# Chunk-selected attention with a gated linear unit: the five-tap convolution on TensorE re-tiled to 64 x 32, and the selection mask applied in 64-row halves

## The chip, the cores and the metric

One core of a Trainium2 chip. The metric is the time of one execution on the device, in microseconds. Before the change it was 196.78 us in the median of three runs (196.16 to 199.24).

## What is computed

The first half is attention in which each query row may only look at six 32-row chunks of keys; the second half is a gated linear unit whose gate is a causal convolution over five rows. Cut to what matters (B, H, S, D = 4, 8, 768, 64; 24 chunks):

```python
ub = sum_d(max(q * k_min[chunk], q * k_max[chunk]))      # bound per query and chunk, causal chunks only
top_chunks = argsort(ub)[..., -6:]
mask = (chunk(j) in top_chunks) & (pos_i >= pos_j)
attn = softmax(where(mask, q @ k.T / 8, -1e9)) @ v
x = attn as [B, S, 512]                                  # the 8 heads side by side
gate = sigmoid(sum_k conv_w[k] * x shifted by k - 4)     # depthwise, five taps
out = (gate * (x @ w_val)) @ w_out
```

## The kernel before

**Pairs.** The 32 (batch, head) attention problems are done in 16 pairs: two heads share the 128 partitions, one in rows 0 to 63 and one in rows 64 to 127. Four pairs make one batch's 512 channels of `x`. For a pair p, in this order: `kn`, `qn`, `vn` are loaded (L517 to L526); K and Q are transposed on TensorE (L534) and copied to f16 as `Kh`, `Qh` by ScalarE (L540, L576); VectorE takes the chunks' minima and maxima (L546); GpSimd makes `KB` of them (L566 to L571); TensorE multiplies the bounds (`ub`, L652 or L667); VectorE finds the sixth largest (`top`) and writes 1 where a chunk is *not* selected into `NS` (`cmp`, L712 to L719); TensorE transposes `NS` (L726), and the copy of that is `MT` (L732, L734).

**Scores.** `score` (L738 to L761) computes K x Q for a pair into banks of PSUM, one bank for each head and each of six column ranges (`BANKS`, in 24 causal 128-blocks), with contraction over 64 rows (L748), and adds a penalty to the chunks that are not selected by a second matmul with the constant `E` (L757). `DUO` takes two ranges at a time; `cmp` writes `NS` twice, 32 columns apart, so that `MT` holds two copies of each head's rows, and four mask matmuls of 32 rows x 128 columns can run for two heads and two banks. ScalarE takes the exponential (L766), GpSimd zeroes the upper triangle of diagonal blocks (L774), TensorE multiplies by V (L797), VectorE normalises into `on` (L805, L806), and a transposing DMA (L827) or, for the last pair, TensorE (L822) makes `xT`, channels on partitions.

**Convolution.** Each pair's convolution is a set of matmuls whose weights are diagonal matrices. `CONV = "QQQQQQQQQQQSSSSQ"` gives each pair one of two ways.
- Q (`convq`, L876 to L885; 12 pairs): weights as f16 high part and low part (m), so 2 x 5 taps; tiles of 64 x 64. `XQ` is `xT` with its two 64-row halves exchanged by two DMAs (L849), so that four tiles work at once; 40 matmuls of 384 columns.
- S (`conv`, L856 to L865; pairs 11 to 14): `xT` is written to a DRAM scratch (L839) and read back four times (L845), which puts four copies of a channel, two of them shifted by three rows, on neighbouring partitions; tiles of 128 x 32, two halves of 12 matmuls.

ScalarE takes the tanh (L889). The weights are made once: `WQ` by ten GpSimd products of 512 elements (L476), `WD` by four of 384 (L445), after small VectorE steps (L416 to L437, L459 to L472). `wval` and `wout` are loaded by two DMAs from GpSimd (`wbig`, L408 to L412).

**Second half.** Once a batch's four `xT` are there: `val` = x @ w_val (L913), `gv` = (tanh + 1) * val (L921), `out` = gv @ w_out (L937), its copy (L944, L947) and the store (L952).

**Order.** Nothing is ordered by hand. `graph` lists the operations with a cost, what they read and write, and a key (`PERIOD` x pair + `OFF` + `DELTA`); `Graph.schedule` runs a list scheduler over TensorE, ScalarE, VectorE, GpSimd and SyncE with eight PSUM banks; the kernel is emitted in the resulting order, engine by engine. `fill` adds dummy matmuls (L1011) in gaps of TensorE planned before 26 us. All loads, exchanges, scratch transfers and stores are issued in one order from SyncE, which stops at the first that has to wait. Buffers per name are in `NBUF` (kn, qn, vn 5; XS, XQ 3; xT 8).

Of the kernel before, what the change touches and what calls it, by code (L numbers as in the profile page):

```python
# [33 lines left out]
XN = S + 6  # L34

# [15 lines left out]

DUO = ((0, 1), (2, 3), (4, 5))
SCORE = [0.68, 0.70, 0.54]
# [3 lines left out]
for _bi, _segs in enumerate(BANKS):  # L57
    for _col, _jt, _q0, _n in _segs:
        for _i in range(_n // 128):
# [5 lines left out]
PERIOD = 12.9223  # L65
OFF = dict(wdg=199.168, wbig=-116.538, cw=-683.48, load=-91.162, ktr=-51.291, qtr=99.521, kev=-172.346,
           qev=175.061, ksm=-204.505, spl=464.719, vc=678.633, ub=-186.285, top=322.7, selT=-163.727,
           sc=-181.883, ex=-292.07, av=82.464, nrm=333.712, tox=-546.25, xs=-141.243, conv=13.848,
           tanh=-338.872, val=266.063, gv=171.155, out=288.504, ev=-184.148)
# [11 lines left out]
CONV = "QQQQQQQQQQQSSSSQ"  # L81

DELTA = dict(
    wdg=(-1.243, -0.346, -5.29, 3.059, -8.51, 0.295, -11.031, 1.615, 2.466, -0.239, -5.796, 0, -2.239, 11.59,
        -0.038, 0),
    wbig=(0, 0.188, -10.953, -0.19, 0.733, -1.414, -3.353, 1.285, -5.523, -4.485, 38.175, 5.823, 4.557,
        -13.478, 0.421, 0),
    cw=(-18.314, -8.891, -8.843, -0.026, -0.2, 7.762, 12.344, 5.613, 0.06, -2.242, -4.873, -3.047, -3.366,
        0.828, -9.749, -0.011),
    load=(0.214, -1.353, 0.394, -9.477, -20.991, -15.326, -0.566, -8.721, 0.066, -10.887, 23.08, 13.879, 6.207,  # L90
        -4.098, -7.797, -2.716),
    ktr=(3.721, -2.57, -4.059, 0.646, -13.55, 0, 0.055, -1.62, -0.373, 0.436, -1.532, 6.05, 2.065, 1.379, 2.36,
        0.267),
    qtr=(-5.316, -3.862, 0.606, 2.517, 0.494, 0.207, -0.25, -17.411, 1.198, 7.239, -4.482, 0.617, -1.715,
        -0.705, 1.938, 2.43),
    kev=(0, -2.085, -0.198, 0.772, 0.854, 1.732, -0.381, -2.561, 0.048, 6.873, -0.748, -3.931, -1.54, -5.598,
        0, 0),
    qev=(-0.006, -7.153, 2.8, -8.078, -1.913, -4.426, -6.52, -0.93, -1.584, 0.557, 6.224, 0.433, 0, 0.167,
        0.325, 1.843),
    ksm=(-0.516, 1.719, 1.719, 0, -8.166, 5.024, -7.553, -5.823, 0, -13.821, -3.788, 0, 0, 0, 6.169, -3.771),  # L100
    spl=(0, 0, 0.913, -1.823, 3.174, 0.698, 2.737, 0, -0.344, -1.736, -3.55, 8.03, 12.699, 0.056, 12.489, 1.296),
    vc=(-5.408, 8.102, -1.641, -3.236, -11.492, -2.331, -9.437, 2.42, -16.561, 6.032, 0, -2.029, 9.507, 2.124,
        11.374, 1.314),
    ub=(0, 5.87, -1.717, -6.846, -10.954, -7.75, -4.319, 18.215, 2.367, -3.332, -1.487, -3.834, 2.838, -3.08,
        -3.376, 6.316),
    top=(0.011, -14.157, -0.748, -6.694, 0, 1.128, -0.085, 25.804, -19.326, 6.323, 7.216, 7.115, 6.031, 0,
        17.873, -1.714),
    selT=(0.159, 4.322, -11.032, -3.664, 2.206, 2.91, 4.105, -0.067, 0, 2.718, -8.959, -6.512, 0.16, 8.002,
        -0.12, -1.732),
    sc=(2.402, 2.062, 3.966, 0.001, -31.282, -1.168, -3.404, 9.113, -1.06, 0.639, 4.728, -3.231, -1.122,  # L110
        -0.658, -0.515, 0.885),
    ex=(-2.337, 0.461, 5.963, 6.189, 0.222, 2.13, 5.144, 9.503, 6.939, 0.624, 0.959, -13.542, -6.471, -4.563,
        6.731, -4.322),
    av=(0.086, -0.585, 2.526, 2.997, -2.315, -1.993, -1.22, 0, 3.593, 0, 0.163, -0.487, -7.862, -6.595, 1.978,
        -0.201),
    nrm=(-6.208, 0.692, -9.254, 2.271, -0.558, 4.28, 2.998, -3.761, 1.41, 1.599, -8.131, 15.962, -6.789,
        -7.511, -3.999, -3.399),
    tox=(-0.124, 4.074, 0.356, 0.146, 0, -8.203, -3.783, -8.724, -14.631, -6.792, 4.598, -8.206, -0.922,
        -1.434, -0.461, 1.278),
    xs=(-2.03, -2.537, 6.003, -3.321, -6.852, 156.074, 8.152, -17.228, -0.596, 0.102, -1.967, -1.865, -3.351,  # L120
        -1.967, -6.798, 4.494),
    conv=(-1.279, -0.745, -0.991, 1.197, -2.443, 4.986, 5.472, 4.646, -0.942, 1.84, 7.166, -0.096, 2.503,
        -1.052, 4.405, 6.594),
    tanh=(2.324, 0.747, -0.277, -2.803, 0, -3.819, -9.599, -8.531, -3.417, -0.893, -3.327, -0.726, -11.212,
        -0.762, 0.19, -5.493),
    val=(9.122, 0, -6.241, -3.696, 12.326, 2.893, 6.691, -2.508, -1.856, -2.108, -6.259, 37.115, 3.96, 9.385,
        10.567, 13.154),
    gv=(0.221, -7.002, -6.129, -3.775, -3.838, 1.864, 0, 7.518, 5.786, 5.443, -1.952, 0.455, 3.175, 0.33,
        -10.961, 5.879),
    out=(1.189, 1.43, -6.802, 3.456, 1.001, 0.92, -7.795, 60.654, -9.234, 0.84, 0.994, -0.377, 1.598, -2.455,  # L130
        -0.186, 1.785),
    ev=(-3.564, -1.25, -5.306, -0.157, 0, -6.542, 10.476, 4.737, 0.526, 6.5, 7.77, 0.056, 0, 0.402, 3.529,
        -0.709),
# [186 lines left out]
def graph(off, period, nbuf):  # L320
# [81 lines left out]

    if "S" in CONV:
        def w_cw():
            t.nc.sync.dma_start(out=t.cw, in_=t.conv_w.rearrange("k (c d) -> (k c) d", d=32))
        G.op("cw", "SP", 0.6, key("cw", 1), w_cw, w=[("cw",)], lat=3.0)

    def w_big():  # L408
        t.nc.gpsimd.dma_start(out=t.wval, in_=t.w_val.rearrange("(ct c) e -> c ct e", c=128))
        t.nc.gpsimd.dma_start(out=t.wout, in_=t.w_out.rearrange("(et e) o -> e et o", e=128))  # L410
    later = []
    later.append(G.op("wbig", "POOL", 2.4, key("wbig", 2), w_big, w=[("wbig",)], dma=6.4))  # L412

    if "S" in CONV:
        def w_rep():
            t.nc.vector.tensor_copy(out=t.cw4, in_=t.cw.unsqueeze(2).to_broadcast([80, 32, 4]))  # L416
        G.op("cwrep", "DVE", 0.6, 11.4, w_rep, r=[("cw",)], w=[("cw4",)])

        def w_tr():
            t.nc.tensor.transpose(out=bank("cwT")[:, 0:80], in_=t.cw4.rearrange("p d b -> p (d b)"),  # L420
                                  identity=t.ident[0:80, 0:80])
        G.op("cwT", "PE", 0.12, 11.4, w_tr, r=[("cw4",), ("ident",)], ps=["cwT"])

        def w_split():
            nc, b = t.nc, bank("cwT")
            v, c4 = nc.vector, t.ident.rearrange("p (c b) -> p c b", b=4)
            v.tensor_reduce(out=t.pm[:, 0:4], in_=t.ident.rearrange("p (c b) -> p b c", b=4), axis=AX.X, op=ALU.add)
            v.tensor_reduce(out=t.id4, in_=c4, axis=AX.X, op=ALU.add)
            v.tensor_tensor(out=t.pm[:, 4:6], in0=t.pm[:, 0:2], in1=t.pm[:, 2:4], op=ALU.add)
            v.tensor_tensor(out=t.pm[:, 6:7], in0=t.pm[:, 0:1], in1=t.pm[:, 1:2], op=ALU.add)  # L430
            v.tensor_tensor(out=t.pm[:, 7:8], in0=t.pm[:, 2:3], in1=t.pm[:, 3:4], op=ALU.add)
            v.tensor_copy(out=t.whi, in_=b[:, 0:80])
            v.tensor_tensor(out=t.wlo, in0=b[:, 0:80], in1=t.whi, op=ALU.subtract)
            v.tensor_scalar(out=t.wlo, in0=t.wlo, scalar1=t.pm[:, 5:6], scalar2=None, op0=ALU.mult)
            v.scalar_tensor_tensor(out=t.wlo, in0=t.whi, scalar=t.pm[:, 4:5], in1=t.wlo, op0=ALU.mult, op1=ALU.add)
            v.tensor_scalar(out=t.wsel, in0=t.wlo[:, 0:48], scalar1=t.pm[:, 6:7], scalar2=None, op0=ALU.mult)
            v.scalar_tensor_tensor(out=t.wsel[:, 0:32], in0=t.wlo[:, 48:80], scalar=t.pm[:, 7:8], in1=t.wsel[:, 0:32],  # L437
                                   op0=ALU.mult, op1=ALU.add)
        G.op("wsplit", "DVE", 2.7, 11.4, w_split, r=[("cwT",), ("ident",)], w=[("wsel",)], ps=["cwT"],
             after=[G.ops[-1]])  # L440

        def w_diag(j):
            def emit():
                sl = slice(12 * j, 12 * j + 12)
                t.nc.gpsimd.tensor_tensor(  # L445
                    out=t.WD[:, sl, :], in0=t.id4.unsqueeze(1).to_broadcast([128, 12, 32]),
                    in1=t.wsel[:, sl].unsqueeze(2).to_broadcast([128, 12, 32]), op=ALU.mult)
            return emit
        for j in range(4):
            G.op(f"wdiag{j}", "POOL", 0.8, 12.3 + 0.1 * j, w_diag(j), r=[("wsel",)], w=[("WD",)])  # L450

    if "Q" in CONV:
# [26 lines left out]
        for m in range(2):  # L479
            for k in range(KSZ):  # L480
                later.append(G.op(f"qdiag{m}{k}", "POOL", 1.0, key("wdg", 2, 0.5 * (m * KSZ + k)), q_diag(m, k), r=[("qw",)],
                                  w=[("WQ",)]))
# [659 lines left out]
```

## Time and profile before

| what | value |
|---|---|
| median of three runs | 196.78 us |
| profiled execution, its own time | 197.75 us |
| its span, first to last instruction | 196.0 us |
| ScalarE exponentials L766 | 192, 88.9 us busy |
| AV matmuls L797 | 672, 28.0 us busy |
| convolution Q matmuls L883 | 480, 21.8 us busy |
| convolution S matmuls L863 | 96, 4.7 us busy |
| K x Q matmuls L748 / mask matmuls L757 | 384, 28.8 us / 352, 17.6 us busy |
| GpSimd products for WQ / for WD | 10, 10.9 us / 4, 3.2 us busy |
| DMAs of kn, qn, vn | 32, 32 and 16, of 192, 192 and 384 KB |

A matmul's duration in the profile is counted until its last result is out, and matmuls overlap, so busy times of lines overlap too and cannot be added; the distance from one start to the next is what a matmul takes of TensorE. A row of tiles written "64*64 64x384" is a weight tile of 64 rows x 64 columns and a moving operand of 64 x 384.

### The profile page before, as it was taken

The numbers are of one execution on the slowest core, as the hardware profiler recorded it, in microseconds if no ns is written. First come the engines' busy times: TensorE is split into PE (matmuls) and PEld (weight loads), VectorE is DVE, ScalarE is ACT, GpSimd is POOL, SyncE is SP. The second block draws the span as 40 slices with busy tenths as digits, with TensorE's granted clock in tenths as the row PEclk, the third lists the DMA queues.
The fourth block names the chain that finished last, engine by engine and source line by source line (L and its number), as shares of the span: only waits on it lengthen the run. The fifth ranks groups of instructions, "written<-read, shape, count | busy, mean of one in ns | idle before, by whom it ended". The sixth has DMA issues, their size and how long they took to land.

```text
span 196.0 us, 7461 instructions
## 1 busy us (share of the span) xinstructions
PE 184.8 (94%) x2926; PEld 118.4 (60%) x2926; DVE 148.3 (76%) x476; ACT 146.7 (75%) x326; POOL 90.4 (46%) x189
## 2 busy tenths in 40 slices
PE   7989898979999999999999999999999997899992
PEld 3666666656757675686675677577656462555540
DVE  6897588979999988879998558998899614062451
ACT  4458999989778879895969897677988977633421
POOL 5589999888445344547262137414363212100000
PEclk9999999999999999999999999999999999999999
DMA  5999999989989998969796998230218839777225
GB/s 134 269 269 207 163 211 205 255 161 225 236 147 222 151 279 190 262 142 222 198 257 181 251 221 162 58 70 2 47 48 251 117 92 282 221 261 251 106 110 211
DMA packets 94917, 36.01 MB, mean 184 GB/s; under 512 B 88226, under 2 KB 91298, under 8 KB 94882
## 3 DMA queue, kind: packets, MB, share of 16 engines
q1 hardware_dynamic: 93826, 34.48, 74.5%
q0 software_dynamic: 1056, 1.05, 3.8%
q8 instruction: 23, 0.38, 0.8%
q14 instruction: 12, 0.10, 0.2%
HBM read 24.16 MB, written 7.08 MB: 159 GB/s over the span
## 4 chain that ended last, share of the span: by engine, by line
PE 74%; DVE 12%; DMA 5%; ACT 4%; SPq 2%; issue 2%; DVEq 0%
PE b L883 10%; PE b L913 10%; PE b L937 9%; PE b L797 9%; PE b L748 8%; PE b L534 8%; PE b L757 5%; PE b L652 5%; DMA xT<-on 3%; DVE km L546 3%; ACT P L766 2%; DMA XS<-scr 2%; PE b L726 2%; PE b L1011 2%; PE b L352 2%; DVE NS L716 2%
## 5 line engine op out<-in xcount | busy, mean ns | idle before, releaser
L766 ACT ACTIVATE P<-b 128x512 f16<-128x512 f32 (+1 forms) x192 | 88.9, 570 | 9.8 <-PE b L757 4.7
L774 POOL TENSOR_SCALAR_AFFINE_SELECT P<-P 128x512 f16<-128x512 f16 (+1 forms) x64 | 33.8, 550 | 60.5 <-ACT P L766 60.4
L546 DVE TENSOR_REDUCE km<-b 128x12 f32<-128x384 f32 x64 | 31.9, 548 | 6.7 <-PE b L534 2.8
L748 PE MATMUL b<-Qh,Kh 64*128 64x128 f16 (+3 forms) x384 | 28.8, 258 | 0.9 <-ACT P L766 0.4
L797 PE MATMUL b<-VA,P 128*128 128x65 f16 x672 | 28.0, 194 | 0.5 <-ACT P L766 0.4
L797 PEld LDWEIGHTS <-P 128*128 128x128 f16 x672 | 24.8, 98 | 4.1 <-issue 1.8
L921 DVE SCALAR_TENSOR_TENSOR gv<-g,b 128x384 f16<-128x384 f32 x32 | 17.5, 550 | 10.2 <-PE b L913 9.1
L913 PE MATMUL b<-xT,wval 128*128 128x384 f16 x128 | 23.8, 326 | 0.0
L937 PE MATMUL b<-wout,gv 128*128 128x512 f16 x96 | 23.5, 379 | 0.0
L947 ACT ACTIVATE osb<-b 128x512 f32<-128x512 f32 x21 | 12.8, 623 | 13.8 <-PE b L937 11.7
L889 ACT ACTIVATE g<-b 128x384 f32<-128x384 f32 x32 | 14.4, 495 | 10.2 <-PE b L883 7.6
L883 PE MATMUL b<-xT,WQ 64*64 64x384 f16 x240 | 21.8, 325 | 0.0
L883 PE MATMUL b<-XQ,WQ 64*64 64x384 f16 x240 | 21.8, 325 | 0.0
L540 ACT ACTIVATE Kh<-b 128x384 f16<-128x384 f32 x32 | 16.2, 520 | 7.0 <-PE b L534 5.2
L748 PEld LDWEIGHTS <-Kh 64*128 64x128 f16 x384 | 12.0, 94 | 12.8 <-issue 11.3
L806 DVE TENSOR_TENSOR on<-b,rcp 128x384 f16<-128x384 f32 x32 | 17.8, 557 | 1.1
L576 ACT ACTIVATE Qh<-b 128x384 f16<-128x384 f32 x32 | 15.7, 531 | 2.7 <-PE b L534 2.7
L757 PE MATMUL b<-MT,E 32*128 32x128 f16 (+4 forms) x352 | 17.6, 259 | 0.0
L883 PEld LDWEIGHTS <-WQ 64*64 64x64 f16 x480 | 12.8, 106 | 6.8 <-issue 2.0
L913 PEld LDWEIGHTS <-wval 128*128 128x128 f16 x128 | 11.5, 98 | 7.9 <-issue 1.3
L622 DVE SCALAR_TENSOR_TENSOR rl<-Qh,ql 128x640 f16<-128x640 f16 x16 | 15.9, 994 | 0.2
L534 PE MATMUL b<-ident,kn 128*128 128x128 f32 x96 | 15.1, 282 | 0.1
(102 smaller groups left out, 320.8 us busy)
## 6 DMA issues: line engine op xcount, KB each, us to landing
kn<-in_k_dram SPq DMA_DIRECT2D x32, 192.0 KB, 3.7
qn<-in_q_dram SPq DMA_DIRECT2D x32, 192.0 KB, 3.7
vn<-in_v_dram SPq DMA_DIRECT2D x16, 384.0 KB, 5.1
out_dram<-osb SPq DMA_DIRECT2D x24, 256.0 KB, 3.1
XS<-scr SPq DMA_DIRECT2D x16, 193.3 KB, 3.3
XQ<-xT SPq DMA_DIRECT2D x24, 96.8 KB, 2.5
scr<-xT SPq DMA_DIRECT2D x4, 193.5 KB
wval<-in_moe_w_val_dram POOLq DMA_DIRECT2D x1, 512.0 KB, 8.6
```

The costliest lines, as they stand in the source:

```text
L534: t.nc.tensor.matmul(out=b[:, j * 128:(j + 1) * 128], lhsT=vv(name, p)[:, 3 * w + j, :], rhs=t.ident, is_transpose=True, start=(j == 0), s ...
L546: t.nc.vector.tensor_reduce(out=vv("km", p)[:, i, w * 12:(w + 1) * 12], in_=bank(("kn", p, w))[:, 0:HB].rearrange("p (c t) -> p c t", t=CH ...
L748: t.nc.tensor.matmul(out=bank(("s", p, bi, hh))[:, col:col + n], lhsT=kh[HP[hh], jt * 128:(jt + 1) * 128], rhs=qh[HP[hh], q0:q0 + n], star ...
L757: t.nc.tensor.matmul(out=bank(("s", p, bi, hh))[:, col + m0 - q0:col + n], lhsT=t.E[rows, jt * 128:(jt + 1) * 128], rhs=mt[rows, m0 - 128: ...
L766: t.nc.scalar.activation(out=t.P[p % 2][hh][bi], in_=bank(("s", p, bi, hh))[:, 0:n], func=AF.Exp, scale=0.125 / QS)
L774: t.nc.gpsimd.affine_select(out=ap, in_=ap, pattern=[[0, n], [1, 128]], compare_op=ALU.is_ge, fill=0.0, base=0, channel_multiplier=-1)
L797: t.nc.tensor.matmul(out=b[:, qt, :], lhsT=t.P[p % 2][hh][bi][:, col:col + 128], rhs=vv("VA", p)[:, hh, jt, :], start=(jt == 0), stop=(jt ...
L806: t.nc.vector.tensor_tensor(out=vv("on", p)[:, :, hh * 64:(hh + 1) * 64], in0=b[:, :, 0:D], in1=rc.unsqueeze(2).to_broadcast([128, NT, D]) ...
L883: t.nc.tensor.matmul(out=bank(("cv", p, r))[HP[c], 0:HB], lhsT=t.WQ[HP[r], k // KSZ, k % KSZ, (p % 4) * 2 + c, :], rhs=x[HP[r], a:a + HB], ...
L913: t.nc.tensor.matmul(out=k[:, 0:HB], lhsT=t.wval[:, ct, et * 128:(et + 1) * 128], rhs=t.xT[:, (4 * b_ + ct) % 8, XL + w * HB:XL + (w + 1) ...
L921: t.nc.vector.scalar_tensor_tensor(out=vv("gv", 4 * b_ + et)[:, sl], in0=vv("g", 4 * b_ + et)[:, sl], scalar=1.0, in1=bank(("val", b_, et, ...
L937: t.nc.tensor.matmul(out=k, lhsT=vv("gv", 4 * b_ + et)[:, s * 128:(s + 1) * 128], rhs=t.wout[:, et, :], start=(et == 0), stop=(et == NCT - 1))
```

## The change

1. `CONV = "RRRRRRRRRRRRRRRQ"`: pairs 0 to 14 use a new way R. The DRAM scratch now holds 64 rows: 32 channel slots for each half of the 768 rows of `x`, so two writes; it is read back twice, into every second partition, so that each channel has two neighbouring rows (the weight's high part on one, its low part on the other). Five taps x four channel groups x two halves of the sequence make 40 matmuls of 384 columns in eight tiles of 64 x 32. `WD` is 80 blocks of 32 columns instead of 48; way S is gone. Pair 15 keeps Q, and `WQ` is made for that pair's two blocks alone.
2. The mask matmuls use the 64 rows of a head at once (tiles of 64 x 128, as K x Q), bank by bank, directly after their K x Q matmul; `DUO` is gone, and `cmp` writes `NS` once.
3. `wbig` is split into `wval` and `wout`, each with its own key, and not before `ksm3` and `ksm4`; `WQ`'s two products come after `ksm4`; the small weight steps have keys of their own.
4. `PERIOD`, `OFF`, `DELTA` and the planner's costs for the changed operations have other values, so that the order changes on every engine.

```diff
-CONV = "QQQQQQQQQQQSSSSQ"
+CONV = "RRRRRRRRRRRRRRRQ"
-DUO = ((0, 1), (2, 3), (4, 5))
...
-    later.append(G.op("wbig", "POOL", 2.4, key("wbig", 2), w_big, w=[("wbig",)], dma=6.4))
+        last.append(G.op(x, "POOL", 1.2, key("wbig", 2 + 2 * i), w_big, w=[(x,)], dma=3.0))
...
+        for j in range(KSZ):
+            later.append(G.op(f"wdiag{j}", "POOL", 1.0, key("wdg", 2, 0.5 * j), w_diag(j), r=[("wsel",)], w=[("WD",)]))
-                out=t.WQ[:, m, k], in0=t.id2.unsqueeze(1).to_broadcast([128, 8, 64]),
+                out=t.WQ[:, m], in0=t.id2.unsqueeze(1).unsqueeze(1).to_broadcast([128, KSZ, 2, 64]),
...
-            for r in range(2):
-                t.nc.vector.tensor_tensor(
-                    out=vv("NS", p).rearrange("p i (s c) -> p i s c", s=2)[:, :, :, CH * r:CH * r + NCH],
...
+            t.nc.vector.tensor_tensor(
+                out=vv("NS", p).rearrange("p i (s c) -> p i s c", s=2)[:, :, :, 0:NCH],
...
+        def score(bi, p=p):
...
+                for si, (col, jt, q0, n) in enumerate(segs):
...
+                    for hh in range(2):
+                        nc.tensor.matmul(out=bb[hh][:, col:col + n], lhsT=kh[HP[hh], jt * 128:(jt + 1) * 128],
...
+                    if masked:
                         for hh in range(2):
...
+                            nc.tensor.matmul(out=bb[hh][:, col + m0 - q0:col + n],
+                                             lhsT=t.E[HP[hh], jt * 128:(jt + 1) * 128],
+                                             rhs=mt[HP[hh], m0 - 128:q0 + n - 128], start=False, stop=last,
...
         def xw(p=p):
-            t.nc.sync.dma_start(out=t.scr[p % 4].rearrange("c (g n) -> g c n", g=4), in_=t.xT[:, p % 8, XL - 4:XL + S + 2])
+            for r in range(2):
+                t.nc.sync.dma_start(out=t.scr[p % 4][32 * r:32 * r + 32].rearrange("c (g n) -> g c n", g=4),
+                                    in_=t.xT[:, p % 8, XL - 4 + HB * r:XL + HB + HB * r])
         def xs(p=p):
-            for blk in range(4):
-                t.nc.sync.dma_start(out=vv("XS", p)[blk::4, 0:n - 3], in_=t.scr[p % 4][:, sh:sh + n - 3])
+            for blk in range(2):
+                t.nc.sync.dma_start(out=vv("XS", p)[blk::2, :], in_=t.scr[p % 4])
...
+        def conv(p=p):
+            x = vv("XS", p)
+            for k in range(KSZ):
+                for g in range(4):
+                    for r in range(2):
+                        t.nc.tensor.matmul(out=bank(("cv", p, r))[32 * g:32 * g + 32, 0:HB],
+                                           lhsT=t.WD[HP[r], k * 16 + (p % 4) * 4 + g, :],
+                                           rhs=x[HP[r], g * XH + k:g * XH + k + HB], start=(k == 0), stop=(k == KSZ - 1))
```

## The prediction

> **What bounds the kernel now.** I read the page first: shares of the engines and the slices.
>
> ```profile
> PE 184.8 (94%) x2926; PEld 118.4 (60%) x2926; DVE 148.3 (76%) x476; ACT 146.7 (75%) x326; POOL 90.4 (46%) x189
> ...
> PE   7989898979999999999999999999999997899992
> ...
> DMA  5999999989989998969796998230218839777225
> ```
>
> TensorE is nearly always busy, but busy includes the drain of each matmul, so I looked at stretches (columns: busy us of PE, PEld, DVE, ACT, POOL with instruction counts, clock, DMA share, GB/s).
>
> ```profile
> 20.00:50.00 30.00, 26.88 (x511) 18.65 (x511) 26.00 (x90) 28.59 (x68) 27.37 (x46) 1.00 1.04 202
> 50.00:75.00 25.00, 24.89 (x485) 17.70 (x484) 23.66 (x81) 19.48 (x45) 11.46 (x28) 1.00 0.99 206
> 100.00:125.00 25.00, 25.00 (x445) 16.17 (x443) 19.11 (x64) 19.57 (x45) 10.94 (x26) 1.00 0.81 192
> 125.00:150.00 25.00, 25.00 (x434) 16.37 (x433) 22.96 (x78) 21.42 (x49) 9.97 (x22) 1.00 0.31 73
> ```
>
> From 20 to 50 us ScalarE is full (28.59 of 30). From 50 to 150 TensorE is full to within 0.1 us of 100, about ten pairs at 10.0 us each. TensorE's waits agree: the longest, 2.0 us for `XS` from the scratch, comes at 167.5 us, and no other exceeds 1.3. So from 50 us to the end TensorE's own time counts. The timeline shows what a matmul takes of it, from start to start:
>
> ```profile
> 55.22 0.32 PE L883 MATMUL b<-xT,WQ 64*64 64x384 f16 x2
> ...
> 55.38 0.33 PE L883 MATMUL b<-xT,WQ 64*64 64x384 f16 x2
> ...
> 55.54 0.33 PE L883 MATMUL b<-xT,WQ 64*64 64x384 f16 x2
> ...
> 55.81 0.61 PE L748 MATMUL b<-Qh,Kh 64*128 64x512 f16 x4
> 56.34 0.39 PE L757 MATMUL b<-MT,E 32*128 32x512 f16 x4
> 56.67 0.45 PE L748 MATMUL b<-Qh,Kh 64*128 64x256 f16 x8
> 57.05 0.34 PE L757 MATMUL b<-MT,E 32*128 32x256 f16 x8
> ```
>
> A round of four 64 x 64 tiles takes 0.162 us (0.16 between the first rows), as long as 384 columns alone; so four tiles do run at once, 3 ns apart. But 55.54 to 55.81 is 0.26: about 0.095 more, and I find 0.09 to 0.10 at nearly every place where the tile shape changes (64 x 128 to 32 x 128: median 0.095 over 48). A way-S round (four tiles of 128 x 32) takes 0.166.
>
> Next the loads, from SyncE's timeline and TensorE's: pair 15's kn, qn, vn are issued here, and kn is first used at 140.82.
>
> ```profile
> 110.72 3.45 SPq L522 DMA_DIRECT2D kn<-in_k_dram  x2
> 115.46 1.27 SPq L522 DMA_DIRECT2D qn<-in_q_dram  x2
> 116.83 0.49 SPq L519 DMA_DIRECT2D vn<-in_v_dram  x1
> ```
>
> The second kn load lands by about 116, so the DMA side, full until 125 us, is 24 us ahead at the end, though only 3 to 7 us ahead (qn) at pairs 5 to 7.
>
> **What the skill says.** "TensorE: Matmul & The Clock Gate", Part 3, has tiles at different positions running concurrently, starts about 4 ns apart; sixteen 32 x 32 tiles gave 10.6 times. The trace agrees for four tiles (3 ns); no run here shows eight. "TensorEngine Tiling (Array Packing)", Tiling Modes, lists eight tiles of 64 x 32, and says that a change of mode, not of tile, drains the array: agreed, 0.095 us. "Trainium Kernel Development and Optimization", Key Constraints: DMAs from all queues share the same 16 engines. The trace agrees in that the share is 1.04 from 20 to 50 us, where `wval` and `wout` from GpSimd load beside SyncE's transfers.
>
> **The change, part by part,** on TensorE first.
>
> *Convolution.* Before: 12 Q pairs x 10 rounds x 0.162 = 19.4 us, 4 S pairs x 6 rounds x 0.166 = 4.0: 23.4. After: 15 R pairs x 5 rounds of eight tiles. No row shows one; bounds: 0.16 (384 columns, fully side by side; below that nothing) and 0.33 (only four at once, S's streams full). I take S's 0.165, since S already feeds four moving streams of 128 rows, as much data as eight of 64, and Q already loads as many weight columns per round (4 x 64 = 8 x 32). 75 x 0.165 = 12.4, plus pair 15's 1.6: 14.0. **-9.4 us.**
>
> *Masks.* Between 50 and 150 us the start-to-start times of L757 add up to 9.1 us for ten pairs; 30 of them end in a shape change (2.85), so 0.63 us a pair stream, four strips at once. After, two strips: the segments of the six banks sum to 320 + 448 + 512 + 512 + 384 + 256 = 2432 columns a head; 512 columns take 0.216 us in L937 (eight in 1.73 on the chain), so 1.03 us. +0.40 a pair, x16: **+6.4 us.** K x Q keeps its columns.
>
> *Shape changes.* Counted in the two built orders of TensorE: 160 before, 115 after (the 48 between K x Q and masks go; single score banks among other work add some). 45 x 0.095: **-4.3 us.**
>
> Sum on TensorE: -7.3 us. Before 50 us, where ScalarE is full, masks (+0.4 x 3.5 pairs) and shape changes nearly cancel and are covered by its waits there; everything of the convolution comes later. If TensorE's cover were gone before 50 us, that would cost 0.5.
>
> *VectorE.* `cmp` falls from 0.72 to about 0.36 us (two instructions to one): -5.8 over 16; the weight steps of 3 us before the first K reduction become about 2.3 later. Not on the path while TensorE is full, and it keeps VectorE's 23.66 of 25 us from becoming the bound: per pair 8.9 - 0.4 = 8.5 of 9.5 us, 89% as now.
>
> *GpSimd.* WQ and WD (10.9 + 3.2) become five products of 512 (1.11 each) and two of 640 (1.39 by size): 8.3; -5.8. Its 27.37 of 30 us before 50 loosens, as do ScalarE's waits for `KB` (2.9 us in all). I take 0; bounds -2.5 and 0. `wval` and `wout`, later, free DMA time (7.5 us) for the first loads and are needed only after 60 us.
>
> *DMA and SyncE.* Q costs 128 packets of 1548 B (0.10 us each over 16 engines: 0.8 us a pair). R writes 256 packets of 776 B and reads 128 of 3104 B: no row; by S's rates (1548 B at 15 GB/s, 6186 B at 21 per engine) 0.8 + 1.2 = 2.0 us; lower 1.5 (each at its undisturbed speed), upper 2.8 (all at the 13.4 GB/s of 256 B packets). I take 2.0. By the last qn load the new order on SyncE has sent 9.5 pairs' transfers, where 9 Q pairs' were sent before: 9.5 x 2.0 - 9 x 0.8 = 12 us later. Of the 24 us of lead, 12 and TensorE's 7 come off; 5 are left. So it is hidden, by that lead; at 2.8 us a pair it would be late by 2 to 3. SyncE issues 16 DMAs more (0.58 each, 9 us); it waits some 75 us now. Behind each scratch read, which waits for its write to land, loads and stores are queued; who waits is first `XS`, then pair 14's convolution: the new order puts about 16 us of matmuls between that pair's AV and its convolution, and transpose, write, read with their issues take 13 to 15 (before: 153.4 to 167.2 on the chain). I add 0.5 for such waits; bounds -2 (before's 2.0 vanishes) and +5.
>
> Sum against the profiled span: 196.0 - 7.3 + 0.5 = 189.2. The median of the runs lies 0.8 above the span (the profiled execution's own time 1.75), so 190.0 us.
>
> **Rivals.**
> 1. *Eight tiles run as four and four.* Nothing speaks against S's bandwidth, but no trace shows eight. Each round then takes 0.33, +12.4 us: 202.4, slower. It decides from a round of 0.256 (no change) and 0.31 (2% slower).
> 2. *The DMA side becomes the bound.* For: share 0.99 to 1.04 up to 75 us, leads of only 3 to 7 us there. Against: 24 us of lead at the end and `wval`, `wout` out of the first loads. With leads gone I price it at 5 us of waits: 195.
> 3. *VectorE or ScalarE keep the old pace.* For: VectorE 95% busy from 50 to 75. Against: -0.36 us a pair there. Half of TensorE's gain is lost: 193.5.
>
> **How the numbers follow.** Main course 0.57 (187 to 192.5 as its own range), rival 1 0.12, rival 2 0.17 (with a long tail), rival 3 0.14. About 2% (192.8, 200.7) is what a measurement of this kernel can tell from no change. Faster: 0.55 of the main course, a little of 2 and 3: 0.62. Slower: most of rival 1 and the tail of 2: 0.14. Same: 0.24. The range reaches from 185.5 (GpSimd's and the wait's lower bounds, -4) to 201: beyond lies most of rival 1.
>
> **What would show it.** Rounds of eight starts 0.16 to 0.17 us apart and 40 in 0.9; shape changes still 0.095; mask and K x Q of one bank with no gap; TensorE's start-to-start time full from 50 us with nearly no wait for `kn`, `qn` or `XS`. I am wrong if rounds take over 0.25, or if TensorE waits for loads after 60 us.

## The result

The kernel after takes 204.24 us in the median of four runs (203.45 to 205.55), the kernel before on the same chip 197.0: the ratio is 1.039, 95% interval [1.030, 1.048]. It is slower by 3.9%; 190.0 was predicted. The profiled execution took 204.88 us, with a span of 203.1.

Ratios here compare, for each kernel, the runs within about 1.5% of its fastest, so a ratio can lie below that of the two medians. Where I turn a difference of ratios into time, 1% is 1.97 us.

### The profile page after: what moved, and what is told of

Read it like the earlier page. It is cut to its first block, busy times and chain, and to the rows that moved or that the text cites. A ratio compares the mean times of both kernels' runs of the same rounds, so it can differ in the third digit from the quotient of the medians.

```text
span 203.1 us, 7574 instructions
## 1 busy us (share of the span) xinstructions
PE 180.6 (89%) x2981; PEld 120.9 (60%) x2981; DVE 142.1 (70%) x456; ACT 144.8 (71%) x326; POOL 86.1 (42%) x182
## 4 chain that ended last, share of the span: by engine, by line
PE 51%; DMA 19%; DVE 12%; ACT 10%; issue 3%; SPq 3%; ACTq 0%; DVEq 0%
DMA qn<-in_q_dram 12%; PE b L920 9%; PE b L896 8%; PE b L738 7%; PE b L525 7%; PE b L781 6%; ACT P L752 6%; PE b L743 5%; PE b L846 4%; DMA XS<-scr 4%; PE b L643 3%; DMA kn<-in_k_dram 2%; SPq L513 2%; ACT Qh L567 2%; DVE km L537 2%
## 5 line engine op out<-in xcount | busy, mean ns | idle before, releaser
L738 PE MATMUL b<-Qh,Kh 64*128 64x128 f16 (+3 forms) x384 | 39.4, 261 | 0.2
L743 PE MATMUL b<-MT,E 64*128 64x128 f16 (+4 forms) x352 | 37.3, 257 | 1.1 <-DVE MT L724 1.1
L781 PE MATMUL b<-VA,P 128*128 128x65 f16 x672 | 26.4, 193 | 0.0
L738 PEld LDWEIGHTS <-Kh 64*128 64x128 f16 x384 | 18.2, 95 | 12.4 <-issue 8.6
L896 PE MATMUL b<-xT,wval 128*128 128x384 f16 x128 | 25.3, 327 | 0.0
L930 ACT ACTIVATE osb<-b 128x512 f32<-128x512 f32 x21 | 12.8, 618 | 16.6 <-PE b L920 11.5
L630 POOL CAST VA<-vn 128x768 f16<-128x768 f32 x16 | 13.7, 866 | 21.7 <-DMA vn<-in_v_dram 12.2
L567 ACT ACTIVATE Qh<-b 128x384 f16<-128x384 f32 x32 | 15.5, 531 | 9.6 <-PE b L525 9.6
L743 PEld LDWEIGHTS <-E 64*128 64x128 f16 x352 | 17.7, 95 | 4.9 <-issue 2.1
L846 PE MATMUL b<-XS,WD 64*32 64x384 f16 x600 | 15.8, 341 | 4.2 <-DMA XS<-scr 4.2
L525 PE MATMUL b<-ident,qn 128*128 128x128 f32 x96 | 14.3, 280 | 5.5 <-DMA qn<-in_q_dram 4.7
L525 PEld LDWEIGHTS b<-ident,kn 128*128 128x128 f32 x96 | 11.3, 151 | 9.2 <-ACT P L752 5.7
```

The source lines that it names most:

```text
L525: t.nc.tensor.matmul(out=b[:, j * 128:(j + 1) * 128], lhsT=vv(name, p)[:, 3 * w + j, :], rhs=t.ident, is_transpose=True, start=(j == 0), s ...
L567: t.nc.scalar.activation(out=vv("Qh", p)[:, w * HB:(w + 1) * HB], in_=bank(("qn", p, w))[:, 0:HB], func=AF.Copy, scale=QS)
L738: nc.tensor.matmul(out=bb[hh][:, col:col + n], lhsT=kh[HP[hh], jt * 128:(jt + 1) * 128], rhs=qh[HP[hh], q0:q0 + n], start=(si == 0), stop= ...
L743: nc.tensor.matmul(out=bb[hh][:, col + m0 - q0:col + n], lhsT=t.E[HP[hh], jt * 128:(jt + 1) * 128], rhs=mt[HP[hh], m0 - 128:q0 + n - 128], ...
L781: t.nc.tensor.matmul(out=b[:, qt, :], lhsT=t.P[p % 2][hh][bi][:, col:col + 128], rhs=vv("VA", p)[:, hh, jt, :], start=(jt == 0), stop=(jt ...
L846: t.nc.tensor.matmul(out=bank(("cv", p, r))[32 * g:32 * g + 32, 0:HB], lhsT=t.WD[HP[r], k * 16 + (p % 4) * 4 + g, :], rhs=x[HP[r], g * XH ...
```

## The profile after

First the page of the kernel after: shares, slices of TensorE, of its clock and of the DMA engines.

```profile
PE 180.6 (89%) x2981; PEld 120.9 (60%) x2981; DVE 142.1 (70%) x456; ACT 144.8 (71%) x326; POOL 86.1 (42%) x182
...
PE   7899899997969589989699999979976999799992
...
PEclk9999999999999889999889999999997999999999
DMA  7999999999876799996999997988979862728055
```

TensorE is busy for 4 us less than before, in a span 7 us longer: its row now has holes (6, 5, 8, 6) in the middle. Its granted clock dips after some of them. That does not make the difference in time: of the four runs the one with a granted clock of 1.000 was the longest, 205.55 us. The DMA row fell to 3 and less about two thirds through the span before; now it stays near full to four fifths of it. The same stretches as in the prediction, same columns (the DMA share is the sum of the packets' times over that of 16 engines; it passes 1 where packets of one engine overlap):

```profile
20.00:50.00 30.00, 27.37 (x504) 21.06 (x503) 27.85 (x102) 27.78 (x67) 25.82 (x44) 1.00 1.25 200
50.00:75.00 25.00, 20.64 (x413) 15.32 (x410) 18.02 (x58) 18.79 (x44) 11.62 (x24) 0.93 0.84 168
...
100.00:125.00 25.00, 25.00 (x451) 16.93 (x449) 20.78 (x65) 20.27 (x47) 10.11 (x22) 0.94 0.93 219
125.00:150.00 25.00, 23.40 (x364) 15.63 (x365) 17.86 (x58) 18.95 (x43) 9.95 (x22) 1.00 0.96 197
```

From 50 to 75 us TensorE has 20.64 of 25 us (24.89 before). From 125 to 150 us the DMA share is 0.96 (0.31 before): transfers that were over by then before are still being made. The chain of waits says for whom TensorE stands (start, duration, what):

```profile
82.18 5.04 DMA qn<-in_q_dram
...
92.59 6.35 DMA qn<-in_q_dram
...
129.60 4.66 DMA qn<-in_q_dram
...
138.87 0.94 PE b L846 x40
...
148.20 5.91 DMA XS<-scr
```

The chain before had 5% of DMA in it, this one 19%, of which `qn` is 12%. The row of L846 is one pair's convolution: 40 matmuls in eight tiles take 0.94 us, so 5 rounds of 0.17 and a shape change of 0.095. Eight tiles do run together. TensorE's own list of waits (us in total, times, longest):

```profile
PE b L525 <- DMA qn<-in_q_dram: 4.7, 5, 1.8
PE b L846 <- DMA XS<-scr: 4.2, 2, 3.0
PE b L525 <- DMA kn<-in_k_dram: 3.0, 3, 2.2
```

No wait for `kn` or `qn` was on this list before. Last, SyncE's timeline for pair 15, as shown before:

```profile
130.17 2.27 SPq L513 DMA_DIRECT2D kn<-in_k_dram  x2
...
140.83 1.71 SPq L513 DMA_DIRECT2D qn<-in_q_dram  x2
...
149.99 0.40 SPq L510 DMA_DIRECT2D vn<-in_v_dram  x1
```

kn of pair 15 is first used at 155.8, 25.7 us after its issue, much as before (30.1). The trouble is earlier. kn of pair 7:

| kernel | kn of pair 7: issue, first use | kn of pair 15: first use | from pair 7's to pair 15's | from there to the end |
|---|---|---|---|---|
| before | 43.8, 57.5 | 140.8 | 83.3 | 55.2 |
| after | 53.3, 59.5 | 155.8 | 96.3 | 47.3 |

In the middle TensorE loses 13.0 us. At the end it gains 7.9; that this is near the predicted 7.3 is chance: the two orders put different work behind that point (72 matmuls of K x Q before, 48 after). At pair 7 the load is issued 6.2 us ahead of its use, where it was 13.7. There TensorE still waits for ScalarE (1.9 us); the first long wait for a load is that for kn of pair 8, 2.2 us at 69.6.

## Experiments

All were timed beside the kernel before. Theory: the bytes of way R on the DMA engines make loads late. Rivals: SyncE's longer list of issues; the round trip through DRAM; the order of the loads; and later, the buffers' addresses. "After" in a diff is the kernel after.

**Without the scratch transfers, and with short ones.** The first leaves out all 60 scratch transfers, the second keeps every one with its waits but moves 16 bytes a descriptor. Both fill `XS` with a constant, so the convolution's values are not the reference's.

```diff
-                t.nc.sync.dma_start(out=t.scr[p % 4][32 * r:32 * r + 32].rearrange("c (g n) -> g c n", g=4),
-                                    in_=t.xT[:, p % 8, XL - 4 + HB * r:XL + HB + HB * r])
+                t.nc.sync.dma_start(out=t.scr[p % 4][32 * r:32 * r + 32].rearrange("c (g n) -> g c n", g=4)[:, :, 0:8],
+                                    in_=t.xT[:, p % 8, XL - 4 + HB * r:XL + 4 + HB * r])
...
-                t.nc.sync.dma_start(out=vv("XS", p)[blk::2, :], in_=t.scr[p % 4])
+                t.nc.sync.dma_start(out=vv("XS", p)[blk::2, 0:8], in_=t.scr[p % 4][:, 0:8])
```

> Leaves out all 60 scratch DMAs of pairs 0 to 14 (writes and reads); the convolution reads XS tiles set once to 0.01, so its result is not x's. The order of everything else is as in the changed kernel. If the scratch transfers (by their bytes or by their place in SyncE's queue) made the loads late, TensorE is full from 50 us and the time is what the prediction summed for TensorE: 187 to 191. If the new order of the other engines is to blame, it stays over 200.

> All 60 scratch DMAs are issued and waited for as in the changed kernel, but each moves 16 bytes a descriptor instead of 776 or 3104 (the rest of XS is set once to 0.01; the convolution's result is not x's). Theory queue (SyncE's issues and waits in order, not bytes, make the loads late): 201 to 205, as the changed kernel. Theory bytes (the 16 DMA engines are short): 188 to 193.

Measured: 190.19 us, ratio 0.967 [0.961, 0.974], and 188.87 us, 0.962 [0.956, 0.968]. The stretches of the one with short transfers:

```profile
50.00:75.00 25.00, 23.45 (x485) 17.48 (x493) 22.74 (x77) 21.55 (x50) 15.97 (x32) 1.00 0.85 157
75.00:100.00 25.00, 25.00 (x453) 16.43 (x438) 22.38 (x67) 21.52 (x49) 11.07 (x24) 1.00 0.79 159
100.00:125.00 25.00, 24.82 (x462) 17.45 (x459) 23.23 (x77) 20.30 (x47) 9.35 (x22) 1.00 1.01 179
125.00:150.00 25.00, 25.00 (x482) 16.70 (x485) 18.93 (x62) 21.52 (x49) 12.48 (x27) 1.00 0.61 155
150.00:175.00 25.00, 24.90 (x438) 15.02 (x423) 11.16 (x33) 15.89 (x37) 3.86 (x8) 1.00 0.31 89
```

From 75 us on TensorE is full again (column PE), and the DMA share falls to 0.61 and 0.31 at the end. The predicted time is there, with all issues and waits in place, though a wait for a short transfer is shorter too: what costs the time is the bytes, not the number of SyncE's issues. Removing the issues as well gives nothing more. From pair 7's first use of kn to pair 15's it now takes 82.3 us (96.3 in the kernel after). TensorE's start-to-start times, its idle gaps over 0.15 us taken out, add up to 176.8 us, for 185.1 before: -8.3, where -7.3 was predicted. These kernels fill `XS` by three memsets on VectorE at the start, and kn of pair 4 is first used 2 to 3 us later than in the kernel after, so their times are, if anything, too long.

**All bytes, no round trip.** The reads come from a constant scratch and do not wait for their own pair's write.

```diff
-                t.nc.sync.dma_start(out=vv("XS", p)[blk::2, :], in_=t.scr[p % 4])
+                t.nc.sync.dma_start(out=vv("XS", p)[blk::2, :], in_=t.scrc)
```

> All bytes and all issues stay, but the reads take a constant scratch tile, so that no read waits for its pair's write to land (the convolution's result is not x's). If the wait for the write inside SyncE's queue is what holds the loads up: 190 to 196. If bytes or the count of issues are: 202 to 205.

Measured: 206.21 us, 1.051 [1.042, 1.059]. No gain: the round trip is not the cause. The run is not clean, because the constant scratch is filled by a memset and a write that stand ahead of the loads of pair 1 in SyncE's order: its kn is issued at 5.4 us for 3.1, and kn of pair 4 is first used at 31.8 for 29.6. That accounts for some 2 us; without them the time would be about that of the kernel after, far from the 190 to 196 that I had expected if the round trip held the loads up.

**Loads first.** kn, qn and vn are moved ahead of scratch, transposing and store DMAs in SyncE's order, as far as their buffers allow (`free` holds the last readers of a load's buffer).

```diff
+        to = max(free, default=-1) + 1
+        while to < i and not (order[to].eng == "SP" and order[to].name[:2] in ("xw", "xs", "xd", "od", "sw")):
+            to += 1
+        if to < i:
+            order.insert(to, order.pop(i))
```

> The changed kernel with each load of kn, qn, vn moved up in SyncE's order to the first place where the planner has its buffer free, past stores, transposes and scratch transfers; nothing left out. Theory queue: the loads are no longer behind waits, 192 to 198. Theory bytes: the same bytes in another order, 201 to 207, with the scratch transfers late in place of the loads.

Measured: 213.48 us, 1.086 [1.077, 1.094].

```profile
PE b L525 <- DVE on L790: 12.3, 1, 12.3
PE b L846 <- DMA XS<-scr: 5.3, 2, 3.1
```

This is longer than either theory said. The waits for loads are gone (0.3 us are left) and larger ones stand in their place. The long one ends with `on`, which had to wait for the transposing DMA that empties its buffer; SyncE issues that DMA at 52.4 us, behind loads alone from 35.0 on. Lead for the loads is taken from what is behind them in the one queue.

**Addresses.** The packets of the loads (256 B each) were slower in the kernel after and in the four kernels made from it so far: in the first 25 us, where no scratch transfer runs yet, 22.6 ns in the mean for the kernel after, 18.2 before. The source and the issue are the same. What differs is where the buffers lie: kn0 starts at byte 81152 of a partition before (317 x 256) and at 75648 after (295.5 x 256). The smaller `WQ` and larger `WD` move it by 5632 B, which is 22 x 256; the odd 128 B come from the small tile `wsel`, which has 80 columns of 4 B instead of 48. So I moved the buffers on by 128 B, to a multiple of 256 B, in the kernel after, and by 128 B off one in the kernel before; a third kernel, with pads of its own, puts `on`, `XS` and `osb` at multiples of 256 B as well.

```diff
+    t.pad0 = tl("pad0", [128, 32])
     t.tiles = {n: [tl(f"{n}{i}", *sh) for i in range(nbuf[n])] for n, sh in shapes.items()}
```

> The changed kernel with one unused 128-byte tile ahead of the load buffers: kn, qn, vn start at multiples of 256 bytes in SBUF, as in the kernel before, instead of 128 past one; the order of all instructions is the same. Theory scratch bytes alone: 202 to 206, and the loads' 256-byte packets stay at a mean of 23 to 24 ns. Theory buffer address (every packet of a load crosses a 256-byte line, and that is what took the DMA side's reserve): packets back at 19 to 20 ns, 190 to 197.

> The kernel before with the same unused 128-byte tile, so that its kn, qn, vn start 128 bytes past a multiple of 256. Theory buffer address: packets at 22 to 24 ns, and its 90% full DMA side falls behind: 199 to 206. Theory scratch bytes alone: 196 to 198, packets at 19.7 ns.

> As the run with aligned loads, and the buffers of on, XS and osb start at multiples of 256 bytes too. Theory buffer address: another 1 to 3 us less than with the loads alone (30 reads of 3104 bytes and 24 stores of 2048 bytes a partition). Theory scratch bytes alone: 202 to 206.

Measured: the kernel after with its loads aligned 199.63 us, 1.010 [1.001, 1.020]; with all buffers aligned 198.79 us, 1.004 [1.000, 1.008]; the kernel before, shifted, 201.23 us, 1.020 [1.011, 1.028]. The load packets took 18.0, 18.0 and 23.5 ns in the first 25 us. For the aligned loads I had expected 190 to 197: the packets are back at their old time, the kernel is not. That aligning the other buffers gains anything is not shown; the two intervals overlap. The DMA queue's line (packets, MB, share of 16 engines over the span) of before, then of before shifted, after, and after with all aligned:

```profile
q1 hardware_dynamic: 93826, 34.48, 74.5%
```
```profile
q1 hardware_dynamic: 93826, 34.48, 84.9%
```
```profile
q1 hardware_dynamic: 97130, 37.28, 87.7%
```
```profile
q1 hardware_dynamic: 97130, 37.28, 84.3%
```

Between the first two the packets and bytes are the same, and the share rises by a seventh. The Trainium skill, "DMA: Bandwidth & Descriptors", section "How a descriptor splits into AXI transactions", says that a descriptor that does not start at a multiple of 256 B costs a further transaction; it speaks of reads. Here the start in SBUF, where the load writes, matters by the same multiple. The packets of 256 B (loads, and the transposing DMAs, about a seventh of them) take 104.8 us of the 16 engines' time before and 126.4 with the shift; 127.3 after and 116.3 with all aligned. So the address is half of what they gained from before to after (22.5 us); the other half (11.5) is there with aligned buffers too, beside R's bytes. Only two offsets, 0 and 128 B, were tried.

**Which pairs' bytes.** On the kernel with all buffers aligned, short transfers for pairs 0 to 7 only, for 8 to 14 only, and for all.

```diff
+    n = 8 if p < 8 else 4 * XH
     for blk in range(2):
-        t.nc.sync.dma_start(out=vv("XS", p)[blk::2, 0:4 * XH], in_=t.scr[p % 4])
+        t.nc.sync.dma_start(out=vv("XS", p)[blk::2, 0:n], in_=t.scr[p % 4][:, 0:n])
```

> All buffers at multiples of 256 B; all 60 scratch transfers, but those of pairs 0 to 7 carry 16 bytes a descriptor (so what their convolutions compute is not the reference's). Theory (bytes that are queued ahead of the loads make the loads late): pairs 0 to 7 are all ahead of the last loads, 16 us of packets come off where the DMA engines are full, and nearly the whole loss goes: 190 to 191.5. Rival (waits for the scratch, after the loads are done, hold the end): pairs 8 to 14 keep theirs, 195 or more.

> The mirror image: scratch transfers of pairs 8 to 14 carry 16 bytes a descriptor, those of pairs 0 to 7 are whole. Theory: of the seven pairs only two or three have their scratch ahead of the last qn load (issued at about 140 us), so at most 4 to 6 us of packets come off where it counts: 193 to 196. Rival (waits for the scratch at the end): nearly the whole loss goes, 190 to 191.5, and more than with the first eight short.

> The fourth corner: all scratch transfers with 16 bytes a descriptor (188.9 with buffers 128 B past a multiple of 256), now with all buffers at multiples of 256 B. Theory (the address makes load packets slower, and that counts only where the DMA engines are the bound): no difference, 188 to 189.5, TensorE being the bound. Rival (the address slows something else as well, such as the engines' own reads): 184 to 186.

Measured: 193.76 us, 0.986 [0.979, 0.993]; 195.8 us, 0.995 [0.992, 0.998]; 190.85 us, 0.971 [0.967, 0.975]. Early bytes cost more than late ones, as expected, but the first eight are not nearly all of it: I expected 191.5 at most. With hardly any bytes the alignment gains nothing: the ratio is 0.971 where it was 0.962 with the other addresses, and the intervals just overlap. Yet the 256 B packets take 104.2 us here and 117.0 there. So the slower packets cost time here only where the DMA engines were near full.

**Way Q for four pairs.** Pair 3's, 7's and 11's block of channels is pair 15's, so `WQ` is there.

```diff
-CONV = "RRRRRRRRRRRRRRRQ"
+CONV = "RRRQRRRQRRRQRRRQ"
```

> Way Q for pairs 3, 7, 11 and 15 in the kernel with all buffers at multiples of 256 B; way R for the other twelve. Pairs 3, 7 and 11 cost TensorE 0.8 us more each (1.64 for 0.83) and the DMA engines 1.2 us less each (0.8 for 2.0). Theory (the DMA engines are the bound until the last loads): 2.4 us of TensorE's are covered by its waits and 3.7 us of the DMA engines' come off: 195 (193.5 to 197), against 198.8 without this edit. Rival (the rest of the loss is not the DMA engines' bytes but waits of the scratch at the end): TensorE's 2.4 us are added: 201.

Measured: 196.37 us, 0.998 [0.995, 1.000], against 1.004 with R for all. Three pairs with twice the TensorE time for their convolution are not slower. It is no faster than the kernel before.

**The same bytes on the old order.** Is it the bytes, or bytes on this order? The kernel before gets one more read of 128 x 3104 B behind each exchange of the first pairs, into an `XS` buffer that nothing reads: some 15 us of packets on top of its own 22, where R has 31 in all. The edit shown is that of the second try.

```diff
+            elif p < 11:
+                t.nc.sync.dma_start(out=vv("XS", p)[:, 0:1552], in_=t.scd)
```

> The kernel before, with one more DMA behind each of the first eleven exchanges: 128 descriptors of 3104 B from a constant scratch into an XS buffer that nothing reads (11 x 1.3 = 14 us of packets, about what way R adds in all; 11 issues more on SyncE; a GpSimd memset and one small write at the start). Theory (DMA time ahead of the loads is the bound; the 24 us of lead at the end say nothing of the middle of the kernel, where loads are 3 to 7 us ahead): TensorE starts to wait for qn at pairs 5 to 9, 199 to 201. Rival (the prediction's step: a lead of 24 us takes 14 us of packets): same as before, 196.5 to 197.5.

> The same with all later buffers 128 B past a multiple of 256 B, so that loads and bytes stand as in the kernel after, on the old TensorE order (201.2 us without the bytes). Theory (the DMA side alone sets the time of the kernel after, and TensorE's gain of 7 us is not seen in it): 204 to 207. Rival (bytes and address are not additive, or TensorE's order adds to the loss): 201 to 202.

Measured: 203.44 us, 1.032 [1.024, 1.041], and 212.56 us, 1.082 [1.074, 1.090]. These two are spoilt: a memset and a write that waits for it stood ahead of the first loads, and kn of pair 4 was used 4 us later (36.6 for 32.7) before any added read was issued. Without that:

> As the kernel before plus 14 us of packets, but without the memset and the write at the start, which held up the first loads by 3 us: the scratch is written from pair 0's own channels behind its exchange, and pairs 1 to 10 read 128 x 3104 B from it into an XS buffer that nothing reads (10 x 1.3 + 1.6 = 15 us of packets, 12 issues more). Theory (14 us of packets ahead of the loads cost time in the middle whatever TensorE's order): 199 to 200.5, kn of pairs 7 to 15 first used 2 to 4 us later against each other than before (83.3 us from pair 7's to pair 15's). Rival (the prediction's step, the lead of 24 us takes them): 196.5 to 197.5, 83.3 us kept.

> The same with all later buffers 128 B past a multiple of 256 B, as in the kernel after, on the old TensorE order (201.2 us without the bytes). Theory (bytes and address are two loads on the same engines, and together exceed what the old order can hide too): 205 to 209. Rival (the old order's lead takes both): 201 to 202.

Measured: 199.63 us, 1.011 [1.008, 1.014], and 207.92 us, 1.054 [1.047, 1.061]. TensorE's waits in the first, then in the second:

```profile
PE b L888 <- DMA XQ<-xT: 1.9, 2, 1.6
PE b L868 <- DMA XS<-scr: 1.9, 1, 1.9
```
```profile
PE b L888 <- DMA XQ<-xT: 5.7, 4, 2.5
PE b L534 <- DMA qn<-in_q_dram: 2.0, 3, 1.2
```

In the first, kn of pair 7 still has 12.6 us from issue to use and that of pair 15 28.3: the old order's lead does hold for the loads, as the prediction said of it. What comes late are the exchanges and `XS`; from pair 7's kn to pair 15's it takes 85.9 us (83.3 without the bytes). My number was met by the median, my reason (late `qn`) was not. With the addresses of the kernel after, the same bytes cost 3.4% in place of 1.1%.

**Giving the new order a lead.** Loads of pairs 6 to 15 earlier by up to 6 or 3 us of the planner's time, never before their buffer is free; and the first of these with four Q pairs.

```diff
+        free = max(order.index(a) for a in G.reads.get((name, p - 5), []))
+        at = max(o.start - us, order[free].end + 0.5)
+        to = free + 1
+        while to < i and not (order[to].eng == "SP" and order[to].start >= at):
+            to += 1
+        if to < i:
+            order.insert(to, order.pop(i))
```

> The kernel with all buffers at multiples of 256 B, with kn, qn and vn of pairs 6 to 15 issued earlier on SyncE: by up to 6 us of the planner's time, but not before 0.5 us after their buffer is free. Nothing else is moved. Theory (the new order issues these loads only some 6 to 8 us ahead of their use, where the old one had 14 to 20; the lead on which the prediction rested was a property of the old order): waits for qn and kn go, 2 to 4 us come back: ratio to before 0.985 to 0.995. Rival (the DMA engines have no time left in the middle, an earlier load makes the scratch later by as much): no gain or a loss, ratio 1.00 to 1.02.

> The same by up to 3 us of the planner's time. Theory: half of the gain of the run with 6 us. Rival: no gain, ratio 1.00 to 1.01.

> Both means together: way Q for pairs 3, 7, 11 and 15 (3.7 us of packets less, 2.4 us of TensorE more), buffers at multiples of 256 B, and the loads of pairs 6 to 15 up to 6 us of the planner's time earlier. Theory: with fewer packets the loads find room, ratio to before 0.98 to 0.99 (without the earlier loads 0.998). Rival (no room): 0.995 to 1.01.

Measured: 212.22 us, 1.077 [1.067, 1.086]; 202.74 us, 1.015 [1.003, 1.028]; 218.03 us, 1.101 [1.090, 1.111]. I had expected gains. With 6 us both are worse than the kernels they were made from (1.004 and 0.998); the one with 3 us can't be told from its own. TensorE's waits with 6 us, and the queue's line of that run:

```profile
PE b L848 <- DMA XS<-scr: 13.8, 2, 7.5
PE b L740 <- DVE on L792: 3.5, 1, 3.5
```
```profile
q1 hardware_dynamic: 97130, 37.28, 75.3%
```

No wait for a load is left, kn of pair 7 has 23 us, and `XS` is late by 13.8 us, while the queue's share is down from 84% to 75%. So over the whole span this loss is not want of DMA time. SyncE's timeline tells what came first: from 73.3 to 85.2 us it issues nothing but loads, twelve in a row. The scratch write behind them goes out at 85.2, its read at 86.5, and TensorE stands for that `XS` until 91.5, the longest of its waits. What stands behind such a row of loads in the one queue comes late; that this is all of the loss is my reading and was not tested further. None of my versions beats both kernels, apart from those that leave the data out.

The eight corners, as ratios to the kernel before. The bytes that are added are not the same in both orders, so rows are compared only within one order; the column of bytes gives the packets of scratch and exchanges in us of 16 engines.

| order | bytes | buffers at 256 B | 128 B off |
|---|---|---|---|
| before | its own (22) | 1 | 1.020 |
| before | 15 more (37) | 1.011 | 1.054 |
| after | short (4) | 0.971 | 0.962 |
| after | R (31) | 1.004 | 1.039 (the change) |

## Why the prediction was wrong

- **TensorE's sum was right in the main.** -7.3 us stood in it; -8.3 was measured with the DMA engines relieved, waits taken out, and the time then was 189 to 190. Convolution: 15.5 us start to start for 25.5, -10.0 where -9.4 was written. K x Q and masks together: 42.5 for 40.5, +2.0, where +6.4 and the 48 shape changes that go (-4.6) gave +1.8.
- **Rival 1, eight tiles as four and four, is refuted** by 40 matmuls in 0.94 us.
- **R's 2.0 us of packets a pair were right** for its own packets: 0.75 for its writes (46.7 ns a packet of 776 B) and 1.3 for its reads (162 ns of 3104 B). SyncE issues 18 DMAs more, not 16.
- **The step that failed is "So it is hidden, by that lead".** It took the lead of 24 us at pair 15 in the old order, subtracted 12 and 7 from it, and kept 5. But in the kernel after, kn of pair 15 is still issued 25.7 us ahead of its first use (30.1 before): that lead was hardly touched, and TensorE waited for loads elsewhere, from pair 8 on. Two things were wrong. First, lead belongs to an order of SyncE, not to the kernel. In the new order kn of pair 7 is issued 6.2 us ahead of its use even when the scratch carries almost nothing (55.0 and 61.2 in the run with short transfers; 11.4 us when its DMAs are not issued at all), so there was nothing to subtract 12 from where the loads are tightest. On the old order the lead of the loads did take the bytes. Second, a term was missing: the packets of 256 B, most of them loads, themselves became slower, by 22.5 us summed over 16 engines (104.8 to 127.3), more than the 9 that scratch and exchanges together added (22.2 to 31.3). The prediction kept the loads' cost as it was. Half of the 22.5 is the address, half goes with R's bytes.
- **Rival 2, the DMA side as the bound, was the mechanism**, and its price of 5 us the size that was off. Bytes: 3.4% (0.971 to 1.004), 6.6 us, or more by what the memsets hid. Address: a further 3.5% (1.004 to 1.039), 6.8 us. Together 13 us for 5. By the medians of all runs the two are 4.3% and 2.4%, with nearly the same sum, so the split is rougher than the total. The leads of 3 to 7 us in the middle of the old order, which the prediction named for this rival, were the ones to read.
- **The 0.5 us for waits of `XS`** was also short: 4.2 us.
- **Smaller slips, without effect on the sum.** The lower end of the range adds up to 185.0 (-2.5 from GpSimd and -2.5 from the wait), not 185.5. And a share of 1.04 from 20 to 50 us does not show `wval` and `wout` beside SyncE's transfers, as the prediction read it: the kernel after has 1.14 from 0 to 20 us and issues these two only at 30.9 and 38.1.
- Whether a better order of SyncE would keep R's gain stays open: of the simple reorderings tried none gained and three made it worse, and none of them re-planned the other engines.

## What to carry to other kernels

A lead of loads is a number of one order: read it at the tightest pair, and in the changed order ask where each load is issued, before any bytes are taken off it. When a change alters the size of any tile, compare the start addresses of the DMA buffers behind it; here 128 B from a small tile of weights made the 256 B packets a fifth slower on the old order and a tenth slower on the new one, and cost 2.4 to 3.5% that the diff doesn't show. To separate bytes from waits, keep every transfer and its semaphores and cut only its length.

## What the runs showed of the hardware

- The start of a load's buffer in SBUF, 128 B past a multiple of 256 B: 23.5 ns in place of 18.2 for a 256 B packet in the first 25 us (kernel before, shifted by nothing but a pad). In these 25 us 98% of the packets took 18 ns or less, and 28% with the shift. Over the whole kernel the median stays at 18 ns in both, and the slowest tenth begins at 28 in place of 18.
- The same packets become slower beside others: with all buffers at multiples of 256 B they took 104.2 us of 16 engines with short scratch transfers and 116.3 with whole ones.
- Eight tiles of 64 x 32 with 384 columns take as long a round as four of 64 x 64: 0.163 us from the start of one round to the next in the median, in the run with short transfers as in the kernel before. Where the shape changes behind the last round, about 0.1 us is added (0.115 behind eight tiles, 0.10 behind four).
- TensorE's granted clock was at half for three stretches of 3.4 us before the last matmul of the kernel after (from 69.1, 99.8 and 154.4 us; hence 0.93 and 0.94 in two of the rows above), each behind 3.4 us of which TensorE stood still for 1.8 to 3.0; the kernel before had none. From 100 to 125 us TensorE is busy for all 25.00 us, in part at the lower clock. No limit can be read from this: 2.0 us of standing still in the kernel before, at 167 us, brought no such stretch.
